# GateLoop and ELU layer on one core: the first unit run straight through, weights converted in single steps, the output layer a round behind, and the rows of w_in permuted

## Chip, cores and metric

The kernel runs on one core of one Trainium2 chip. The metric is the device time of one execution in microseconds (us), the median of several runs. Engine names are those of the profile: PE (TensorE matmul), PEld (its weight load), DVE (VectorE), ACT (ScalarE), POOL (GpSimd), SP (SyncE). The letter q behind a name is the engine's sequencer.

## The reference

A gated linear recurrence with complex gates is followed by a two-layer network with ELU.

```
q, k, v, a_re, a_im : (4, 8, 768, 48) float32;  w_in (384, 2048), w_out (2048, 384) float64
mag = sqrt(a_re^2 + a_im^2);  a = (a_re + i a_im) * min(mag, .999) / (mag + 1e-6)
for t:   S = a_t * S + k_t v_t^T          # S complex, (4, 8, 48, 48)
         y_t = q_t . Re(S)
x   = y as (3072, 384)                    # the 8 heads of 48 side by side
h   = x @ w_in ;  g = where(h > 0, h, exp(min(h, 0)) - 1)
out = g @ w_out                           # (3072, 384) float32
```

## The kernel before

The work is cut into 12 units of 2 x 128 tokens. Per unit the kernel computes log and angle of the gates on ACT and DVE (squares, logarithms, angles), sums them over time with matmuls (turns, decays), takes sines (waves), multiplies q and k (gated), transposes them on PE and forms scores, states and values. The result y is moved by DMA from "two heads of 48 to a block of 64" into the dense layout of x (the seam). Then come 8 pieces of hidden layer and 8 pieces of output layer. A round has 16 slots. In each slot the stages of several units are issued side by side. The account below takes an engine's instructions in their order of issue, as the traces show them at the places that matter: in x_qfirst, the inputs of qg are there by 456.53 us, but qg starts on DVE only at 459.60, behind the g that was issued before it and started at 458.99; in the changed kernel, the squares start on ACT at 503.47, behind the copy of o at 503.09.

The weights are float64 and arrive as pairs of 32-bit words. DVE and POOL make float32 of them:

```python
    def load_weights(dst, src):            # one block of 512 (w_in) or 384 (w_out) columns, 28 blocks
        ...
        nc.sync.dma_start(out=w.rearrange("p n two -> p (n two)"), in_=src)
        lo, hi = w[:, :, 0], w[:, :, 1]
        ...                                                   # four steps on DVE
        nc.gpsimd.tensor_tensor(out=p, in0=p, in1=f, op=ALU.add)
        nc.vector.tensor_scalar(out=hi, in0=hi, scalar1=EXP, ...)
        nc.vector.scalar_tensor_tensor(out=dst, in0=hi, ..., in1=p, ...)

    def gated(u):
        for key, by in (("k", "F"), ("q", "E")):
            g = x[by]
            nc.gpsimd.tensor_tensor(out=g, in0=x[key], in1=g, op=ALU.mult)
            ...
            eng = nc.gpsimd if key == "k" else nc.vector
            eng.tensor_tensor(out=o, in0=g..., in1=x["cs"], op=ALU.mult)      # kg, qg

    def seam(u):                           # ten transfers
        for h in range(H):
            e = 0
            while e < D:
                i, r = divmod(h * D + e, C); n = min(D - e, C - r)
                nc.sync.dma_start(out=x[ds(r, n), i], in_=y[ds(h % 2 * HP + e, n), h // 2])
                e += n
```

The schedule spreads a unit's gate stages over three rounds, and its two layers run in a fourth:

```python
    A = [(1, squares), (4, logarithms), (9, angles), (10, carried)]
    BB = [(2, turns), (4, decays), (9, waves), (10, gated)]
    CC = [...]                             # transposes, scores, states, values; (13, seam)
    M = [hidden(u, f) ... 8 pieces] + [project(u, n, f, f + 4) ... 8 pieces]
    for step in range(NU + 3):
        for s in range(SLOTS):
            for late, stage in ((2, CC), (1, BB), (0, A)):
                u = step - late
                ...                        # the stages of this slot
            if step < 3:
                load_weights(...)          # one block a slot
            if step >= 3:
                M[s](step - 3)
```

## Time and profile before

| | before |
|---|---|
| median of 4 runs | 916.67 us (916.38 to 917.34) |
| span of the profiled run | 918.7 us |
| PE busy / idle | 716.1 / 202.6 us |
| first MLP matmul | 197.4 us |
| a steady round | 62.0 us |

The page, the groups and the chain are read in the prediction below. Two more views of the kernel before will be needed. The first is a table by stretch: length, busy time of each engine with its instructions in brackets, then PE's granted clock (1.00 is full), the DMA share and GB/s.

```profile
0.00:231.39 231.39, 62.43 (x508) 47.83 (x508) 126.16 (x212) 67.50 (x90) 74.38 (x60) 0.69 0.38 88
231.39:880.00 648.61, 621.43 (x4723) 453.82 (x4723) 171.60 (x238) 295.25 (x454) 152.62 (x99) 0.99 0.22 40
```

In the first 231 us PE does 62 us of work. In the next 649, some 10.5 rounds, it is idle for only 27 (2.6 a round) and its mean clock is 0.99.

The second is PE in order of time in a late round: start, length, instruction, and in square brackets the idle time ahead of it with what ended it.

```profile
324.69 0.67 PE L797 MATMUL mlp<-x,w_in 128*128 128x256 f32 x2 [0.69 <-DMA x<-y]
326.67 1.99 PE L797 MATMUL mlp<-x,w_in 128*128 128x256 f32 x8 [1.30 <-DMA x<-y]
```

The idle time of a round lies mostly here, in short pieces: the hidden layer of a unit waits for the transfers of its own seam.

### The profile page before, as it was taken

Reading aid. Unit: us, or ns where it says so; the run is one execution under the profiler, and the core shown is the slowest. Engines: PE = TensorE matmul, PEld = TensorE weight load, DVE = VectorE, ACT = ScalarE, POOL = GpSimd, SP = SyncE. Lnnn points to the kernel's source line nnn. Section 1 sums busy time; section 2 is a strip of 40 time slices with the busy share of each in tenths; the row PEclk is TensorE's granted clock in tenths of the full one; section 3 lists DMA queues with packets and bytes.
Section 4 is the critical chain, followed back from the end, with each engine's and each line's share of the span. In section 5 each row is a group of like instructions: output and inputs, shape, how many; then the busy total and the mean of one; then the engine's idle time right before and its main releaser. Section 6 shows DMA issues by size and latency. Waiting matters only on the chain.

```text
span 918.7 us, 13005 instructions
## 1 busy us (share of the span) xinstructions
PE 716.1 (78%) x5346; PEld 523.7 (57%) x5346; DVE 301.9 (33%) x454; ACT 369.8 (40%) x555; POOL 227.0 (25%) x159
## 2 busy tenths in 40 slices
PE   0100002749999999899999999999999999999997
PEld 0000002538667677576676676776766767778684
DVE  2777875314233232133142331331422312112020
ACT  2310302617437257165273381562733714433040
POOL 1322425222302312313233123132330230110000
PEclk9955556659999999999999999999999999999999
DMA  8243143230142212311411422124113021010100
GB/s 210 60 169 103 20 136 68 37 69 3 34 86 37 48 40 37 76 12 35 87 20 22 83 36 56 33 35 86 25 23 76 3 54 33 2 35 2 35 2 20
DMA packets 177485, 47.04 MB, mean 51 GB/s; under 512 B 165720, under 2 KB 173832, under 8 KB 177416
## 3 DMA queue, kind: packets, MB, share of 16 engines
q1 hardware_dynamic: 177096, 46.09, 24.7%
q8 instruction: 44, 0.72, 0.3%
q14 instruction: 25, 0.20, 0.1%
q0 software_dynamic: 320, 0.03, 0.0%
HBM read 36.55 MB, written 4.79 MB: 45 GB/s over the span
## 4 chain that ended last, share of the span: by engine, by line
PE 48%; POOL 14%; issue 12%; SPq 10%; DVE 10%; DMA 4%; ACT 1%; POOLq 0%; DVEq 0%
PE mlp L797 25%; PE mlp L813 12%; SPq L783 5%; POOL kg L689 4%; SPq L509 3%; POOL wp L553 3%; PE w L704 2%; PE w L712 2%; POOL F L686 2%; POOL E L686 2%; PE w L733 2%; DMA x<-y 2%; DVE wf L543 2%; DVE wp L550 2%; PE y L762 1%
## 5 line engine op out<-in xcount | busy, mean ns | idle before, releaser
L797 PE MATMUL mlp<-x,w_in 128*128 128x256 f32 x1152 | 277.9, 392 | 30.1 <-DMA x<-y 23.6
L797 PEld LDWEIGHTS mlp<-x,w_in 128*128 128x128 f32 x1152 | 218.3, 195 | 73.7 <-issue 18.7
L813 PE MATMUL mlp<-w_out,g 128*128 128x384 f32 x768 | 258.5, 490 | 0.0
L813 PEld LDWEIGHTS mlp<-w_out,g 128*128 128x128 f32 x768 | 143.2, 190 | 92.7
L804 DVE SCALAR_TENSOR_TENSOR g<-ee,mlp 128x512 f32<-128x512 f32 x96 | 64.3, 685 | 271.6 <-ACT ee L803 271.6
L802 ACT ACTIVATE ee<-mlp 128x512 f32<-128x512 f32 x96 | 56.9, 593 | 150.9 <-PE mlp L797 149.1
L704 PE MATMUL w<-ident,qg 128*96 128x128 f32 x192 | 27.2, 288 | 107.6 <-DVE qg L689 107.6
L745 POOL TENSOR_TENSOR S<-S,T 96x384 f32<-96x384 f32 x40 | 33.0, 825 | 273.2 <-DVE S L744 252.4
L819 ACT COPY o<-mlp 128x384 f32<-128x384 f32 x24 | 11.5, 479 | 213.8 <-PE mlp L813 213.8
L704 PEld LDWEIGHTS w<-ident,qg 128*96 128x96 f32 x192 | 21.9, 132 | 112.7 <-DVE qg L689 99.2
L581 POOL TENSOR_TENSOR m<-m,e 128x768 f32<-128x768 f32 x12 | 21.7, 1812 | 175.7 <-ACT e L580 175.7
L803 ACT ACTIVATE ee<-ee 128x512 f32<-128x512 f32 x96 | 60.5, 630 | 2.8
L553 POOL TENSOR_TENSOR wp<-wp,wf 128x384 f32<-128x384 f32 (+1 forms) x28 | 32.1, 1145 | 100.5 <-DVE wp L550 97.6
L628 PE MATMUL w<-th,sum_turns 128*128 128x384 f32 x48 | 19.6, 534 | 43.3 <-ACT th L611 43.3
L689 DVE TENSOR_TENSOR qg<-E,cs 128x1536 f32<-128x1536 f32 x12 | 21.1, 1758 | 93.0 <-POOL E L686 93.0
L733 PEld LDWEIGHTS w<-vn,kg 64*96 64x96 f32 x704 | 37.3, 172 | 17.7 <-issue 9.6
L733 PE MATMUL w<-vn,kg 64*96 64x48 f32 x704 | 40.5, 257 | 7.6 <-DVE z L636 7.6
L597 DVE SCALAR_TENSOR_TENSOR l<-m,e 128x768 f32<-128x768 f32 x12 | 23.6, 1968 | 66.1 <-ACT e L593 66.1
L705 ACT COPY qt<-w 96x512 f32<-96x512 f32 x48 | 25.8, 584 | 40.7 <-PE w L704 40.7
L689 POOL TENSOR_TENSOR kg<-F,cs 128x1536 f32<-128x1536 f32 x12 | 41.6, 3463 | 0.9
L744 DVE TENSOR_TENSOR S<-w,S 96x384 f32<-96x384 f32 x40 | 22.1, 552 | 51.1 <-PE w L733 35.6
L628 PEld LDWEIGHTS w<-th,sum_turns 128*128 128x128 f32 x48 | 9.9, 210 | 47.7 <-ACT th L611 43.3
(65 smaller groups left out, 730.8 us busy)
## 6 DMA issues: line engine op xcount, KB each, us to landing
w<-in_moe_w_in_dram SPq DMA_DIRECT2D x12, 512.0 KB
w<-in_moe_w_out_dram SPq DMA_DIRECT2D x16, 384.0 KB
ar<-in_a_re_dram SPq DMA_DIRECT2D x24, 192.0 KB
ai<-in_a_im_dram SPq DMA_DIRECT2D x24, 192.0 KB
q<-in_q_dram SPq DMA_DIRECT2D x24, 192.0 KB
k<-in_k_dram SPq DMA_DIRECT2D x24, 192.0 KB
vn<-in_v_dram SPq DMA_DIRECT2D x24, 192.0 KB
out_dram<-o SPq DMA_DIRECT2D x24, 192.0 KB
```

The costliest lines, as they stand in the source:

```text
L553: nc.gpsimd.tensor_tensor(out=p, in0=p, in1=f, op=ALU.add)
L686: nc.gpsimd.tensor_tensor(out=g, in0=x[key], in1=g, op=ALU.mult)
L689: eng.tensor_tensor(out=o, in0=g.rearrange("p n h d -> p (n h) d").unsqueeze(2).to_broadcast(shape), in1=x["cs"], op=ALU.mult,)
L704: nc.tensor.transpose(t[:, h], x[key + "g"][:, n, h0 + h], ident)
L733: nc.tensor.matmul(g[:, h], lhsT=x["kg"][ts(c, L), n, h], rhs=vn[u % 2][ts(c, L), n, h, 0:D], start=True, stop=True,)
L745: nc.gpsimd.tensor_tensor(out=new_s, in0=new_s, in1=wide, op=ALU.mult)
L783: nc.sync.dma_start(out=x[ds(r, n), i], in_=y[ds(h % 2 * HP + e, n), h // 2])
L797: nc.tensor.matmul(t[:, e], lhsT=w_in[:, i, ts(f + e, C)], rhs=x["x"][:, i], start=(i == 0), stop=(i == NI - 1),)
L802: nc.scalar.activation(out=e, in_=t, func=AF.Relu, scale=-1.0)
L803: nc.scalar.activation(out=e, in_=e, func=AF.Exp, scale=-1.0)
L804: nc.vector.scalar_tensor_tensor(out=x["g", f // 4][:, f % 4 : f % 4 + 2], in0=e, scalar=-1.0, in1=t, op0=ALU.add, op1=ALU.max)
L813: nc.tensor.matmul(x["o"], lhsT=x["g", f // 4][:, f % 4, ts(n, C)], rhs=w_out[:, f], start=(f == 0), stop=(f == NF - 1),)
```

## The change

The intent is to give PE its first work early and to hide the seam. It has four parts:

1. Unit 0 runs alone and straight through, its POOL products on DVE; weights are converted in its gaps.
2. The conversion is a generator: one DVE instruction at a time, in larger blocks (1024 and 768 columns), with the addition on DVE.
3. A unit goes through all its gate stages in one round, its hidden layer runs in the next, and its output layer half in the one after and half at the start of the one after that. So output pieces of earlier units lie between the seam and the hidden pieces that need it.
4. The rows of w_in are permuted so that 48 of each 64 rows of y are already in place: ACT copies them into x, and six short transfers move the two remaining heads.

```diff
-        nc.gpsimd.tensor_tensor(out=p, in0=p, in1=f, op=ALU.add)
+        yield nc.vector.tensor_tensor(out=p, in0=p, in1=f, op=ALU.add)
 ...
+    def products(u):
+        return nc.vector if u == 0 else nc.gpsimd
 ...
     def seam(u):
-        ...                                            # ten transfers, as above
+        for j in range(2):
+            for i in range(NI):
+                nc.sync.dma_start(
+                    out=x["x"][ds(j * HP + D, G), i], in_=x["y"][ds(j * HP + i * G, G)]
+                )
 ...
-    A = [(1, squares), (4, logarithms), (9, angles), (10, carried)]
-    BB = [(2, turns), (4, decays), (9, waves), (10, gated)]
+    GATE = [
+        (0, squares), (1, logarithms), (3, angles), (3, carried), (4, turns), (5, decays),
+        (6, waves), (7, gated),
+    ]                              # then transposes, scores, states, values in slots 9 to 15
+    GATE.append((SLOTS, seam))
+    MLP = {4 + m: hidden piece m (8 pieces)};  MLP[28 + 4 * n + m] = project piece (8 pieces)
+
+    fetches(1)                     # first block of weights
+    load_qk(0)
+    fetches(1)
+    load_v(0)
+    fetches(1)
+    load_a(1)
+    fetches(1)
+    after = {logarithms: 3, turns: 4, waves: 4, gated: 2}
+    for at, fn in GATE:
+        fn(0)
+        ...
+        converts(after.get(fn, int(9 <= at < SLOTS)))
+    for step in range(NU + 2):
+        for s in range(SLOTS):
+            ...                    # gate stages of unit step + 1
+            if step == 0:
+                fetches(int(s < 8))
+                converts(5 if s < 4 else 3)
+            if step == 1:
+                fetches(s % 2)
+                converts(3)
+            for u, m in ((step - 2, s + 2 * SLOTS), (step - 1, s + SLOTS), (step, s)):
+                if 0 <= u < NU and m in MLP:
+                    MLP[m](u)
```

(Cut: sizes, names and sharing of buffers; two transfers in place of four for the chunk ends; a few short forms in place of loops.) A unit's hidden pieces stand in slots 4 to 11 of its round, its output pieces in slots 12 to 15 of the next round and 0 to 3 of the one after.

## The prediction

Two of its trace readings, in full: at 698.25 us PE's clock went to half for 3.41 us, behind 1.93 us of idle time since 694.84; and 0.42 and 0.69 us (512 columns), 0.35 and 0.56 us (384) are weight steps on DVE in the kernel before, the first of each pair with a constant alone, the second with two tensors.

> **What bounds the kernel now.** I read the page first (busy shares, then the 40 slices), then the chain of waits, then the groups of the first 200 us, then one late round in order of time.
>
> ```profile
> PE 716.1 (78%) x5346; PEld 523.7 (57%) x5346; DVE 301.9 (33%) x454; ACT 369.8 (40%) x555; POOL 227.0 (25%) x159
> ...
> PE   0100002749999999899999999999999999999997
> ...
> DVE  2777875314233232133142331331422312112020
> ...
> PEclk9955556659999999999999999999999999999999
> ```
>
> PE is idle for about nine slices of 23 us, with its clock at half, and is then full to the end. The first 200 us belong to DVE, which makes the float64 weights float32. The groups of these 200 us show the same:
>
> ```profile
> L557 DVE SCALAR_TENSOR_TENSOR w_in<-w,wp 128x512 f32<-128x512 uint32 x12 | 11.5, 956 | 13.8 <-POOL wp L553 13.8
> ...
> L704 PE MATMUL w<-ident,qg 128*96 128x128 f32 x24 | 4.9, 373 | 107.6 <-DVE qg L689 107.6
> ```
>
> Each of the 28 weight blocks hands one addition to POOL and waits for it. In time order, a 512-wide block takes 4.43 us and a 384-wide one 3.58, together 12 x 4.43 + 16 x 3.58 = 110 us. These blocks stand in DVE's order ahead of the gate work of unit 0. PE waits 107.6 us for its first transposes, and the first MLP matmul starts at 197.4.
>
> From there on the chain gives the cost of a round on PE, at full clock:
>
> ```profile
> 607.80 2.58 PE mlp L813 x8
> 610.38 1.08 PE w L712 x32
> ...
> 614.24 1.54 PE w L733 x32
> ...
> 640.16 2.59 PE mlp L797 x12
> 642.75 1.29 PE w L628 x4
> ```
>
> The hidden layer is 8 x 2.59 = 20.7 us, the output layer 8 x 2.58 = 20.6, and the gates 14.9 (transposes 3.8, turns and decays 2.6, scores 2.2, states 3.1, values 3.3): 56.2 us. Successive rounds begin their output layer 62.0 us apart (seven rounds, 297.23 to 731.30). So a round idles 5.8 us, mostly at the seam: "SPq L783" has 5.3% of the chain, ten transfers issued at 0.62 us each.
>
> [...]
> - [...] in the stretches below (PE busy first, granted clock third from the end), some 2 us of idle time in pieces was enough, and the clock came back by 702. After an idle start at 154.0 it fell only at 158.9.
>
> ```profile
> 696.00:698.00 2.00, 0.67 (x2) 0.30 (x2) 0.00 (x0) 0.00 (x0) 0.00 (x0) 1.00 0.26 69
> 698.00:702.00 4.00, 3.85 (x12) 2.99 (x13) 0.00 (x0) 0.16 (x1) 0.00 (x0) 0.57 0.76 148
> 702.00:704.00 2.00, 2.00 (x14) 1.85 (x12) 0.00 (x0) 1.97 (x3) 0.00 (x0) 1.00 0.01 3
> ```
>
> - [...] the 128x1536 product takes 3.46 us on POOL (kg) and 1.76 on DVE (qg).
> - [...] 0.42 us against 0.69 at 512 columns, 0.35 against 0.56 at 384.
> - [...] The trace has the 1283 ns; the next activation begins 1.29 us after the load did[...].
>
> **Part 1: unit 0 straight through.** From the arrival of a_re: ACT starts its squares at 6.2 as now. With the products on DVE (768 columns, 0.82 us each) and no weight block in between, t is ready near 16.5 and the angles at 17.4 (now 43.3). Turns and decays at half clock, the three sines and the four products bring qg to about 35 (now 147). Transposes, scores, states and values at half clock add about 21 us, and the seam (six transfers instead of ten, 3.6 us to issue, 2 to land) puts x at about 61.
>
> **Part 2: the weights.** Scaling the two widths linearly: a constant step costs 0.154 + 0.53 ns a column, the others 0.154 + 1.05. An input part of 1024 is 3 x 0.69 + 4 x 1.23 = 7.0 us, six are 42; an output part of 768 is 3 x 0.56 + 4 x 0.96 = 5.5, eight are 44. That is 86 us against 110, since the addition stays on DVE. Of the 98 steps, 23 lie in unit 0's gaps, 56 in round 0, 19 in round 1. Transfers (12.6 MB at the 233 GB/s of the first 20 us) take 54 us in all and arrive in time.
>
> **Part 3: round 0 and 1.** The order of instructions puts 20 weight steps (20 us) on DVE ahead of the rounding of unit 1's turns, behind a unit 1 that itself waits for ACT and POOL. So hidden's activations start near 84. The other 36 steps (30 us), eight g (5.5) and the gates (7.6) keep DVE to about 127. Round 1 has no output layer ahead of its turns: PE waits some 19 us for the logarithms and the weight steps among them. Work 45.9, two waits of 19 and 5, a cold clock: it ends near 200. By then the new kernel is about 60 us of PE work ahead of the old one, which only begins its first hidden layer.
>
> **Part 4: the steady rounds, where I expect a loss.** The seam now has four output-layer pieces (10.3 us) to hide behind and leaves the path: gain 5.8. But a unit now runs through all its gate stages in one round. Two chains become longer than the PE work beside them.
>
> First: squares stand on ACT behind the copy of o, which waits for the last output-layer piece of slot 15. From there: copy 0.5, squares 1.6, POOL addition 1.8, then the chain that the trace shows from the first logarithm to t:
>
> ```profile
> 656.16 0.84 ACT L589 ACTIVATE m<-m 128x768 f32<-128x768 f32 x1
> ```
>
> ```profile
> 664.32 0.96 DVE L601 SCALAR_TENSOR_TENSOR x<-lr,x 128x768 f32<-128x768 f32 x1 [1.71 <-POOL x L595]
> ```
>
> 9.1 us in all (the two lines are ACT's and DVE's), then arctan 0.85 and the carried row 1.0: 15.1 us. PE has 10.3 us to do before the turns: it waits 4.8.
>
> Second, from the turns: turns 1.3, first hidden piece 2.6, relu, table load and exp 2.6, four E/F 1.6, second piece's relu and exp 1.2, load and three sines 4.0, then kg 3.46 and q*E 1.8 on POOL and qg 1.76 on DVE: 20.5 us. PE has five hidden pieces, turns and decays: 15.6. It waits 5.0. After it, 30.9 us of work runs without a wait that I can find.
>
> A round is then 15.1 + 20.5 + 30.9 = 66.5 us, against 62.0. A wait of 5 us will often halve the clock for one 3.4 us window, sometimes two, losing 2 us: at 0.7 of the waits, 2.8 a round, so 69.3. Six table loads a round instead of four are counted in the chains.
>
> **Sum.** 200 to the end of round 1; 9 x 69.3 = 624; rounds without gates 41.3 + 20.6 + 10.3 = 72; a tail of 6.4 as now (912.3 to 918.7); first and last units' missing states -4: 898. I take 895: the two waits are more likely to overlap with something that I missed than to be longer.
>
> **Rivals.**
> - *PE stays dense.* If ACT, POOL and DVE run ahead so that the two waits shrink to the 5.8 us of now, rounds are 62, and the end is 200 + 558 + 72 + 6 - 4 = 832. For it: all three have much idle time. Against: [...] squares stand behind the o copy.
> - *Everything saved at the start is given back.* If each wait cools the clock for two windows, 3.4 us each, rounds are 73, and the end is about 932. For it: after the gap at 385 the clock stayed low from 387.5 to 394. Against: the three other drops of the steady part lasted about 3.5 us.
> - *DVE bound longer at the start.* If rounds 0 and 1 take 15 us more, from shared waits with POOL (the l step took 1.85 instead of 0.95), the result is about 910.
> - *Transfers late.* Only the fifth and sixth input part are fetched after the first seam; they land near 67 and 71 and are used at 68 and 76. A few us at worst.
>
> **Range and chances.** The start is good to 10 us, the rounds to 2 us each over nine: 868 to 922. The bound for faster by 2% is 898.6, close to my middle: faster 0.53, same 0.43, slower 0.04.
>
> **What would show it.** First MLP matmul near 70 to 77 instead of 197.4; DVE 80% full until about 127; no POOL addition of weights. In a late round two PE waits: before the turns, released by DVE's carried row or ACT's arctan, and before the qg transposes, released by DVE qg, about 5 us each, with half clock after many; none from x. Period 66 to 71. I am wrong if a late round takes under 63 us (the chains overlap in a way that I missed), or if the first output layer is not through by 215 (then DVE or the weights' transfers bound the start).

## The result, and the profile after

The changed kernel takes 941.5 us (median of 4 runs, 940.73 to 941.79) against 916.67 of before. The ratio is 1.0269 (95% interval 1.0251 to 1.0286): slower, and outside the predicted range. Here and below a ratio is the mean time of one kernel's fast runs over that of the other's fast runs in the same rounds, so it is not quite the ratio of the medians. Outputs were right. The profiled run spans 939.7 us at a mean clock of 0.898; before it was 918.7 at 0.912.

The page after, its busy line and its slices of 23.5 us:

```profile
PE 744.2 (79%) x5346; PEld 549.4 (58%) x5346; DVE 311.1 (33%) x390; ACT 400.2 (43%) x600; POOL 186.8 (20%) x125
...
PE   2053772798798798798798799799789789879997
...
PEclk9576795899899899899899989989989989889999
```

PE has exactly as many matmuls as before, 5346, and is busy 28.1 us longer with them (744.2 against 716.1). Its idle time is 195.5 us against 202.6. The span is 21.0 us longer: 28.1 us more for the same matmuls, less 7.1 us of idle time. The slices show where: PE starts early as intended, but then every third slice is a 7, and PEclk dips with it to the end. Before, both were flat. The stretches say the same:

```profile
0.00:231.39 231.39, 126.13 (x1081) 96.42 (x1081) 148.95 (x171) 98.73 (x140) 45.26 (x34) 0.79 0.50 92
231.39:880.00 648.61, 564.68 (x4083) 418.63 (x4084) 157.47 (x209) 293.29 (x446) 141.54 (x91) 0.93 0.19 33
```

At 231 us the new kernel has done 573 matmuls more than the old one. In the next 649 us it does 640 fewer: it is idle for 84 us instead of 27, at a clock of 0.93 instead of 0.99. The head start is gone.

The groups name the waits (busy, mean ns of one, then idle time just before and its main releaser):

```profile
L660 PE MATMUL w<-n,sum_turns 128*128 128x384 f32 x48 | 29.8, 769 | 95.9 <-DVE n L649 63.2
...
L735 PE MATMUL w<-ident,qg 128*96 128x128 f32 x192 | 36.2, 351 | 77.3 <-DVE qg L720 77.3
```

Turns (L660) and qg transposes (L735) hold 173 us of the idle time between them. The hidden layer's matmuls (L827) have 0.0 us of idle time before them, where they had 30.1, of which the transfers of x ended 23.6: the seam is off the path. One late round of PE in order of time:

```profile
518.05 2.25 PE L660 MATMUL w<-n,sum_turns 128*128 128x384 f32 x4 [4.67 <-DVE n L649]
...
540.28 1.94 PE L735 MATMUL w<-ident,qg 128*96 128x128 f32 x8 [4.78 <-DVE qg L720]
...
557.44 0.64 PE L735 MATMUL w<-ident,kg 128*96 128x128 f32 x4 [0.47 <-DVE S L775]
...
589.72 2.25 PE L660 MATMUL w<-n,sum_turns 128*128 128x384 f32 x4 [4.67 <-DVE n L649]
```

The round is 71.67 us long, and holds 9.9 us of idle time in two waits and a small third. The trace records when the clock changes. In stretches cut at these changes, the second wait reads:

```profile
535.79:539.20 3.41, 0.00 (x0) 0.00 (x0) 1.18 (x2) 1.96 (x4) 2.65 (x2) 1.00 0.00 0
539.20:542.61 3.41, 2.33 (x10) 2.17 (x11) 2.22 (x3) 0.93 (x2) 0.00 (x0) 0.50 1.00 180
542.61:546.02 3.41, 3.41 (x10) 2.69 (x9) 0.00 (x0) 0.23 (x1) 0.00 (x0) 0.50 0.35 51
```

The clock is at half for 6.83 us here (539.20 to 546.02), of which 5.74 lie behind the end of the wait at 540.28. Behind the other wait it is at half for 3.41 us (518.72 to 522.13), all of them busy. If work at half clock takes twice as long, the two waits lose 2.87 + 1.71 = 4.58 us a round. This is an estimate from these lengths and the granted 0.50 (the eight qg transposes take 1.94 us here and 1.08 at full clock in x_warm, a factor of 1.8); x_warm below measures the loss.

In the traces of the kernel before and of the changed one, all 15 and 49 changes of the clock lie within 1 ns of a grid of steps of 3.413 us, with its own offset in each trace. In the changed kernel, from 231 us to the last matmuls, 17 full-clock steps held 2.47 us or more of PE idle time, and each was followed by a step at half clock; seven held 1.90 to 1.93 us, and none of these was. In the kernel before, four steps with 1.67 to 2.08 us were followed by one at half clock, and three with 1.52 to 1.57 were not. These are counts of two traces, and no limit is read from them.

Last, the start. The chain of waits of the first stretch, start and length of each link:

```profile
17.66 2.94 PE w L660 x4
...
22.08 7.24 DMA carry<-n
29.40 0.85 ACT n L707
...
36.60 6.35 DMA ends<-n
42.97 0.97 DVE n L717
43.97 1.77 DVE qg L720
```

Turns of unit 0 start at 17.66, near the predicted 17.4. Then two small transfers follow: "carry" (3 KB) takes 7.24 us and "ends" (6 KB) 6.35 us. Both hold the rest up, because the next instruction overwrites what they read (the absolute value in place of the angle, q*E in place of E).

### The profile page after: what moved, and what is told of

Same layout as the page of the kernel before. It is cut to its first block, busy times and chain, and to the rows that moved or that the text cites. A ratio compares the mean times of both kernels' runs of the same rounds, so it can differ in the third digit from the quotient of the medians.

```text
span 939.7 us, 12807 instructions
## 1 busy us (share of the span) xinstructions
PE 744.2 (79%) x5346; PEld 549.4 (58%) x5346; DVE 311.1 (33%) x390; ACT 400.2 (43%) x600; POOL 186.8 (20%) x125
## 4 chain that ended last, share of the span: by engine, by line
PE 51%; issue 12%; DVE 11%; ACT 9%; POOL 6%; DMA 6%; SPq 5%; POOLq 0%; DVEq 0%; ACTq 0%
PE mlp L827 18%; PE mlp L843 16%; PE w L735 6%; SPq L815 3%; PE w L660 3%; PE w L743 2%; POOL n L627 2%; DVE qg L720 2%; DMA vn<-in_v_dram 2%; POOL n L717 2%; PE w L764 2%; PE y L793 2%; ACT ee L832 2%; DMA w<-in_moe_w_in_dram 2%; ACT n L687 2%
## 5 line engine op out<-in xcount | busy, mean ns | idle before, releaser
L827 PE MATMUL mlp<-x,w_in 128*128 128x256 f32 x1152 | 292.8, 415 | 0.0
L827 PEld LDWEIGHTS mlp<-x,w_in 128*128 128x128 f32 x1152 | 244.2, 215 | 47.1 <-issue 5.8
L660 PE MATMUL w<-n,sum_turns 128*128 128x384 f32 x48 | 29.8, 769 | 95.9 <-DVE n L649 63.2
L735 PE MATMUL w<-ident,qg 128*96 128x128 f32 x192 | 36.2, 351 | 77.3 <-DVE qg L720 77.3
L735 PEld LDWEIGHTS w<-ident,qg 128*96 128x96 f32 x192 | 27.4, 161 | 84.3 <-DVE qg L720 75.9
L660 PEld LDWEIGHTS w<-n,sum_turns 128*128 128x128 f32 x48 | 11.3, 258 | 106.5 <-issue 67.4
L801 ACT COPY x<-y 128x384 f32<-128x384 f32 x24 | 11.5, 478 | 137.1 <-PE y L793 137.1
L629 DVE SCALAR_TENSOR_TENSOR n<-n 128x768 f32<-128x768 f32 x12 | 21.1, 1756 | 108.7 <-ACT n L625 108.7
L720 POOL TENSOR_TENSOR kg<-n,cs 128x1536 f32<-128x1536 f32 x11 | 37.9, 3450 | 41.7 <-issue 38.3
L717 POOL TENSOR_TENSOR n<-k,n 128x768 f32<-128x768 f32 x11 | 19.9, 1806 | 72.2 <-ACT n L687 72.2
L736 ACT COPY kt<-w 96x512 f32<-96x512 f32 x48 | 26.4, 577 | 16.0 <-PE w L735 16.0
```

What stands on the lines that cost most here:

```text
L660: nc.tensor.matmul(t, lhsT=sum_turns, rhs=x["th"][:, n].rearrange("p h d -> p (h d)"), start=True, stop=True,)
L717: products(u).tensor_tensor(out=g, in0=x[key], in1=g, op=ALU.mult)
L720: eng.tensor_tensor(out=o, in0=g.rearrange("p n h d -> p (n h) d").unsqueeze(2).to_broadcast(shape), in1=x["cs"], op=ALU.mult,)
L735: nc.tensor.transpose(t[:, h], x[key + "g"][:, n, h0 + h], ident)
L736: nc.scalar.copy(out=o[:, h0 : h0 + 4], in_=t)
L827: nc.tensor.matmul(t[:, e], lhsT=w_in[:, i, ts(f + e, C)], rhs=x["x"][:, i], start=(i == 0), stop=(i == NI - 1),)
```

## The experiments

Two theories were at odds after the result. **The clock**: the waits are as predicted, but each halves the clock for longer than was counted. **Hidden extra work or waits**: something else in the round takes 2.4 us more than 69.3. A third question was the start. The kernels below are the changed kernel with one edit each unless it says otherwise. They ran in three calls on two chips, and the kernel before was run beside them: its medians were 917.48, 917.89 and 918.55 us. The changed kernel itself was not run again; its ratio to before is 1.0269, and comparisons between versions below are of periods in the traces or of these ratios. The outputs of all ten were right.

### x_warm: PE kept busy in the two waits

```diff
+    def warm(u, n):                     # units 2 to 11 only
+        j = ps.tile([C, C // L, 512], FP32, tag="y", bufs=1, name="y")
+        for _ in range(n):
+            nc.tensor.matmul(j[:, 0, 0:256], lhsT=ident, rhs=w_in[:, 0, 0:256], start=True, stop=True)
...
+        if key == "q" and n == 0: warm(u, 9)         # ahead of the qg transposes
...
+        warm(u, 9)                                   # ahead of the turns
```

(Shortened.) The added matmuls compute nothing that is used, and no producer of the real work is touched. They share a PSUM buffer with y, but neither they nor y wait for it in the trace.

> The changed kernel with nine junk matmuls (3.9 us at full clock) put on PE in each of the two waits of a round, before the turns and before the first transposes, for units 2 to 11; they read finished weights and write an unused part of PSUM. My account of a round of 71.67 us: 56.2 work, waits of 4.67, 4.78 and 0.47, and about 5.2 lost because PE's clock is halved for 3.4 to 6.8 us after each of the two waits (I had put 2.8 for this). If so, the waits' lengths on the chain stay, the low clock goes, a round takes 66 to 67 us and the kernel about 890 us. Rival: the slow stretch after a wait is not the idle time's doing[...]: then the round stays at 71 or more and the time at 940 or more.

Measured: 896.61 us (896.18 to 897.9), ratio 0.9768 [0.973, 0.9807]. One late wait on PE in order of time, and, one round earlier, the stretch behind the same wait:

```profile
516.21 1.08 PE L749 MATMUL w<-ident,qg 128*96 128x128 f32 x8 [0.92 <-DVE qg L722]
```

```profile
448.00:452.00 4.00, 3.08 (x19) 2.73 (x19) 2.18 (x3) 1.07 (x2) 0.00 (x0) 1.00 0.98 183
```

The round is 67.17 us. Nine added matmuls take 4.05 us and 0.92 is left of the wait: together 4.97, so the chain that ends at qg is as long as before (4.78). Only the clock has changed. It is 1.00, and the same eight transposes take 1.08 us instead of 1.94. More work made the kernel about 45 us faster, some 4.5 us in each of ten rounds, close to the estimate of 4.58. The clock theory is shown. The other falls: what is left, 67.17, is within a microsecond of the 66.5 of the prediction's sum without a clock penalty, and 0.47 of the difference is the small third wait.

### x_warm5: fewer added matmuls

```diff
-WARM_T, WARM_Q = 9, 9
+WARM_T, WARM_Q = 5, 5
```

> As the run with junk matmuls in both waits of a round, but five instead of nine (2.2 us at full clock), so that some 2.5 us of each wait stay idle. The full junk gave 896.6 us and a round of 67.17 without low clock, none gave 941.5 and 71.67. [...] If an idle stretch of some 2.5 us is enough often (in the kernel before, about 2 us in pieces was enough four times in nine), part of the loss stays: 905 to 930 us.

Measured: 908.57 us (906.49 to 909.99), ratio 0.9877 [0.9832, 0.9921]. The five matmuls take 2.32 us and leave 2.44 us idle before the turns and 2.64 before the transposes. Two stretches that each begin about when the turns do, in two successive rounds:

```profile
504.00:508.00 4.00, 3.56 (x15) 2.77 (x16) 2.62 (x5) 0.00 (x0) 0.00 (x0) 1.00 0.83 174
...
572.00:576.00 4.00, 4.00 (x11) 2.71 (x10) 2.23 (x4) 0.00 (x0) 0.41 (x1) 0.57 0.98 202
```

The idle time ahead of both is 2.44 us. Behind the first the clock stays full, behind the second it is near half. So with these shorter waits the penalty comes in some rounds and not in others, and not behind the three longer waits of 2.64 us from 435 to 600 us (before 457.88, 525.03 and 593.88; the eight transposes behind each take 1.08 us). The clock changes at 572.07 and 575.48. In steps of 3.413 us counted from there, the wait before 571.60 lies whole in one step (568.66 to 572.07), the one before 504.44 has 1.80 us in one step and 0.64 in the next, and the one before 525.03 has 1.89 and 0.75. The result lies between x_warm and the changed kernel.

### x_early: squares and logarithms in the round before

```diff
-        (0, squares), (1, logarithms), (3, angles), ...
+        (-3, squares), (-2, logarithms), (3, angles), ...
-            for late, shift in ((0, SLOTS), (1, 0)):
+            for late, shift in ((0, SLOTS), (1, 0), (2, -SLOTS)):
```

Squares stand in slot 13 of the round before, no longer behind the copy of the finished output. In the changed kernel ACT shows that order:

```profile
503.09 0.48 ACT L849 COPY o<-mlp 128x384 f32<-128x384 f32 x1 [2.12 <-PE mlp L843]
503.47 0.85 ACT L611 ACTIVATE n<-ar 128x768 f32<-128x768 f32 x1
```

> The changed kernel with squares and logarithms of a unit moved three slots back into the round before (slots 13 and 14 instead of 0 and 1), nothing else. My account: the wait before the turns (4.67 us, and some 1.8 us of half clock) exists because the chain from squares to the carried row takes 15 us and starts behind the o copy with 10.3 us of PE work left. Started three slots earlier it has over 20 us: the first wait goes, a round takes about 65 us, the kernel about 865 us. Rival: ACT, POOL and DVE are so full in slots 13 to 15 (values, scores, states) that the chain delays these instead: a round stays above 69 and the time above 920.

Measured: 881.31 us (879.3 to 882.49), ratio 0.9602 [0.9564, 0.964].

```profile
485.19 1.45 PE L660 MATMUL w<-n,sum_turns 128*128 128x384 f32 x4
505.67 1.94 PE L735 MATMUL w<-ident,qg 128*96 128x128 f32 x8 [4.79 <-DVE qg L720]
```

The turns no longer wait and run at full clock (1.45 us instead of 2.25). The second wait is as it was. The round is 64.86 us, 6.8 shorter than 71.67: the wait of 4.67 plus 2.1 us of clock. The first wait's cause, that the logarithm chain begins only behind the copy of o, is shown.

### x_qfirst: the products of q ahead of those of k

```diff
-        for key, by in (("k", "F"), ("q", "E")):
+        for key, by in (("q", "E"), ("k", "F")):
```

POOL then makes q*E before it makes kg, which takes 3.46 us.

> The changed kernel with the order of the gated products swapped: q*E and qg before k*F and kg, nothing else. My account: the wait before the first transposes (4.78 us, and some 2.9 us of half clock after it) exists because qg stands behind kg's 3.45 us and k*F's 1.8 us on POOL. With q first, qg is ready before PE gets to it, kg still in time for its own transposes: the second wait goes, a round takes about 64 us, the kernel about 860 us. Rival: the wait only moves to kg's transposes 3.6 us of PE work later, or to the store of the chunk ends that reads E before it is overwritten: then a round loses less than 3 us and the time stays above 910.

Measured: 916.72 us, ratio 0.998 [0.9939, 1.002]; round 68.26 us. The wait shrank from 4.78 to 2.84 us and did not vanish. The round lost 3.4 us where 7.7 were expected, and the time is the rival's (above 910), though the cause is neither of the two that the rival named. All engines in order of time tell why:

```profile
458.33 0.63 ACT L833 ACTIVATE ee<-ee 128x512 f32<-128x512 f32 x1
...
458.99 0.69 DVE L834 SCALAR_TENSOR_TENSOR g<-ee,mlp 128x512 f32<-128x512 f32 x1 [5.74 <-ACT ee L833]
...
459.60 2.13 DVE L720 TENSOR_TENSOR qg<-n,cs 128x1536 f32<-128x1536 f32 x1
...
461.78 1.94 PE L735 MATMUL w<-ident,qg 128*96 128x128 f32 x8 [2.84 <-DVE qg L720]
```

The product qg stands in DVE's order behind the g of a hidden piece. That g waits 5.74 us for an exp, and the exp stands on ACT behind two sines, the absolute value between them and a table load of 1.28 us (the recorded texts count three sines). With POOL out of the way, a second chain of nearly the same length ends the wait.

### x_both: the two edits together

The diff is the sum of the last two.

> The changed kernel with both repairs: squares and logarithms three slots earlier and q's products before k's. The two alone gave 881 and 917 against 941.5 us; the round was 71.67 us as changed, 68.26 with q first and 64.86 with the early squares, which are 21, 20 and 19 times 3.413 us. With q first a wait of 2.84 us is left (qg stands on DVE behind the g of hidden piece 2, whose exp stands on ACT behind the sines). So together: work 56.2, that wait of about 2.8, the 0.47 before kT, and a cold clock after some of the waits only: a round of 60 to 61.4 us (18 windows of 3.413 would be 61.4), and 881 - 10 x 4 = about 840 us. Rival (the two waits are not separate: removing one lengthens the other): a round of 64 and 870 us or more.

Measured: 858.48 us (856.18 to 862.45), ratio 0.9352 [0.931, 0.9393]. The round is 62.0 us with one wait of 2.84 us (3.19 in the first round shown). Behind it the eight transposes take 1.26 to 1.94 us in all seven rounds from 246 to 626 us, against 1.08 at full clock. Three of these were cut finer: the clock is at half for 3.41 us from 374.85 and from 436.29, and for 6.83 from 497.73. The expected 840 us had it fall after some of the waits only. Two small edits, neither of which removes any work, turn the change from 2.7% slower to 6.5% faster. The gains of the two single edits (6.7 and 2.9 points of the ratio) nearly add up to the 9.2 found together.

### x_start: weights fetched behind the small transfers of unit 0

```diff
-    load_v(0)
-    fetches(1)
-    load_a(1)
-    fetches(1)
 ...
     for at, fn in GATE:
         fn(0)
+        if fn is decays:
+            load_v(0)
+            fetches(1)
+            load_a(1)
+            fetches(1)
```

> The changed kernel with v of unit 0, weight part 2, a of unit 1 and weight part 3 issued after unit 0's decays instead of before its squares. My account of the 16 us by which the start came later than I predicted: qg of unit 0 (45.7 instead of 35) waits until the 6 KB store of the chunk ends, issued at 36.6 and landed at 42.97, has read E, because 3 MB of weights and inputs stand ahead of it on the sync queue. Moved behind it, qg is ready near 36 and everything after it 8 to 9 us earlier: about 932 us. Rival: DVE's weight steps set the start anyway (PE waited 8.7 us for the rounding of unit 1 behind them), so that the time moves by under 3 us.

Measured: 931.64 us (931.04 to 933.23), ratio 1.0152 [1.0111, 1.0192].

```profile
35.27 1.94 PE L735 MATMUL w<-ident,qg 128*96 128x128 f32 x8 [12.18 <-DVE qg L720]
```

The first transposes start at 35.27 instead of 45.78; "ends" now takes 1.73 us from issue to landing instead of 6.35. The gain of about 10 us stays to the end: turns of the third and fourth unit start at 149.09 and 220.82, in the changed kernel at 159.21 and 231.39. So 10 of the 16 us that the start missed were these two transfers behind the bulk of the weights. Most of it is not the transfer itself: SP issues "ends" at 24.47 us, in the changed kernel only at 36.60, after the loads that stand before it. The other 6 were not taken apart. A candidate, not shown, is DVE: the 98 weight steps took 95.5 us in the changed kernel instead of the predicted 86, and the nine longest (1.5 to 2.6 us) all ran while a POOL instruction did (the longest of the 67 that did not took 1.23).

### y_seam: the kernel before with part 4 alone

```diff
-        x["y"] = new("y", 1, [C, NP, GT])
+        x["x"], x["y"] = new("x", 2, [C, NI, GT]), new("y", 1, [C, GT])
 ...                                        # two copies and six transfers, as in the change
-            (w_in[:, i, f : f + WC], moe_w_in[ts(i, C), ...])
+            (w_in[:, i, f : f + WC], (i, words * f, words * (f + WC)))    # permuted rows
```

> The kernel before with one part of the change: w_in's rows permuted so that three of four head pairs are copied straight into x and only six transfers of 16 rows remain, in place of ten transfers; schedule, weights' steps and all else as before. My account: in the kernel before a round of 62.0 us has 56.2 of work, and most of its idle 5.8 us is the wait of hidden for x (23.6 us in the table over the rounds, plus the half clock after some of them). With four transfers less (2.5 us of issue) most of it goes: a round of 58 to 59.5 us and 875 to 895 us. Rival: the wait moves to qg or to g, as these were nearly as late: 905 us or more.

Measured: 890.63 us (889.2 to 891.52), ratio 0.9703 [0.9675, 0.973]. Rounds take 58.43 us instead of 62.0. From 231 to 850 us PE is idle for 7.6 us and its clock is 1.00. Of the waits only two short ones are left:

```profile
451.97 0.91 PE L656 MATMUL w<-l,sum_logs 128*128 128x384 f32 x2 [0.20 <-DVE S L750]
...
464.87 2.86 PE L802 MATMUL mlp<-x,w_in 128*128 128x256 f32 x12 [0.67 <-DVE g L809]
```

Part 4 is sound by itself: it is worth 27 us, 3%. What the whole change lost must come from the other three parts, or from how the parts act together.

### x_near: the output layer in its own round

```diff
-                if 0 <= u < NU and m in MLP:
+                if 0 <= u < 2 and m in MLP:
                     MLP[m](u)
+            for u, m in ((step - 1, s + SLOTS), (step, s)):
+                if 2 <= u < NU:
+                    m += SLOTS * (m >= 12)     # pieces after slot 11 come a round later, as a whole
+                    if m in MLP:
+                        MLP[m](u)
```

> The changed kernel with the output layer of units 2 to 11 in the unit's own round (slots 12 to 15 and 0 to 3 of the next), so that one part of the change, the output layer a round behind, is undone where the weights allow it. My account: the same number of output-layer pieces stands in the same slots, so both waits (4.67 and 4.78 us) and the round of 71.67 us stay: 941 us, within 5. Rival: g of the last hidden piece is not ready when the output layer starts, and PE waits 2 us or more in every round, or the other way round the later layer costs something: the time moves by more than 10 us.

Measured: 934.88 us (933.9 to 935.04), ratio 1.0186 [1.016, 1.0211]. Both waits (4.67 and 4.78) and the round (71.6) are as in the changed kernel. The 6.6 us are fewer than the changed kernel's time but more than was expected of this edit; the round in which the two orders meet holds extra output pieces. Where the output layer's pieces come from, this unit or the one before, is not what makes the steady rounds long.

### z_front and z_front2: all gate stages moved forward

```diff
-        (0, squares), (1, logarithms), (3, angles), (3, carried), (4, turns), (5, decays), (6, waves), (7, gated),
+        (-5, squares), (-3, logarithms), (-1, angles), (-1, carried), (0, turns), (1, decays), (3, waves), (4, gated),   # z_front
+        (-4, squares), (-2, logarithms), (-1, angles), (-1, carried), (2, turns), (3, decays), (4, waves), (5, gated),   # z_front2
```

Both include the edits of x_qfirst and x_start. The second also has three weight steps in each slot of round 0 instead of five in the first four slots.

> A version meant to be better than both: the changed kernel with the front of the gate chain taken apart again, squares at slot -5, logarithms -3, angles -1, turns 0, decays 1, waves 3, products 4 (q first), transposes still at 9; and the small transfers of unit 0 ahead of the weights as in the run that gave 931.6. Between squares and turns lie about 17 us of PE work and 10 us more of other work, between turns and the transposes 23 us against chains of 15.1 and 20.5: both waits go, with the clock losses after them, and so do the waits for unit 1's and unit 2's turns at the start (8.7, 15 and 21 us in the changed kernel). A round of 57 us, the end of round 1 near 176 instead of 216, in sum 176 + 9 x 57 + 72 + 6 = about 767 us. Rival: with PE full, ACT or DVE in-order waits take the place, a round of 60 or more: over 800 us.

Measured: 862.42 us (857.46 to 864.83), ratio 0.9378 [0.9335, 0.9421], far from what was hoped. Two new waits took the place of the old ones. In each round PE waits for POOL:

```profile
523.54 1.81 POOL L626 TENSOR_TENSOR n<-ar,n 128x768 f32<-128x768 f32 x1 [8.35 <-ACT n L624]
525.43 2.39 POOL L627 TENSOR_TENSOR n<-ai,n 128x768 f32<-128x768 f32 x1
...
530.23 1.74 PE L793 MATMUL y<-qt,S 96*48 96x64 f32 x28 [3.66 <-POOL S L776]
```

The two products of the logarithms, moved into slot 13, now stand on POOL just ahead of the products of the states, and the carried chain of states reaches PE 3.66 us late. And in round 0, with the gates early, the hidden layer stood behind 20 weight steps on DVE: one wait of 22.40 us, and another of 13.19 in the next round.

> The better version again, with the two new waits of the last one mended. There the logarithms' two POOL products stood ahead of the state products of the same round, so that values waited 3.66 us for S (round 63 to 64 us), and unit 1's first g stood behind 20 weight steps (22.4 us). Now squares at slot -4, logarithms at -2 (behind the states of slot 14), angles -1, turns 2, decays 3, waves 4, products 5, and three weight steps a slot in round 0 instead of five in its first four. Waits left in a round: 0.47 before kT and perhaps 1 us: 57 to 58.5 us without low clock; end of round 1 near 180: 180 + 9 x 58 + 78 = about 780 us. Rival: an in-order wait that I haven't seen takes the place again: a round of 61 or more and over 820 us.

Measured: 797.68 us (797.5 to 799.07), ratio 0.8677 [0.864, 0.8715]. This is the fastest version, 13% faster than the kernel before. Its slices:

```profile
PE   1456682789999999999999999999999999999996
...
PEclk9676895889999999999999999999999999999999
```

From about 180 us on PE is full. The clock is 1.00 from 200 to 700 us, and 0.9 or more in every slice of the page from 179 us on. A round takes 57.9 us, of which only 0.47 is a wait. PE is busy 708.6 us with its 5346 matmuls, 36 less than in the changed kernel.

No run has the changed kernel with the old seam. What parts 1 to 3 would cost alone stays open.

## Why the prediction was wrong

It said 895 (868 to 922) and gave "slower" a chance of 0.04; 941.5 came, slower. Point by point:

- **What bounds the kernel** was right: PE at full clock has 56.2 us of work a round. With the clock kept up, x_warm's round less its waits and added matmuls is 67.17 - 10.2 = 57.0.
- **The seam** leaves the path: right (0.0 us of idle time on L827). Its size was not: "a round idles 5.8 us" was got by subtracting modelled work from the period. The trace has 2.6 us of idle time a round before, and y_seam gains 3.6 a round.
- **The weights**: right in kind. Steps at 1024 columns take 0.69 and 1.22 to 1.31 us, none are on POOL, and there is no wait on a weight transfer in the steady part. In all they took 95.5 us, not 86, and DVE was 72% full to 127 us, not 80%.
- **The two waits**: right in place, releaser and size. Before the turns 4.67 us against 4.8, before the qg transposes 4.78 against 5.0. A third, 0.47, was not seen. x_early and x_qfirst confirm both chains, the second only in part: the sum was computed through POOL, and a second chain through ACT and DVE, only 1.9 us shorter, was not looked for. The sizes are in part luck: the listed terms add up to 14.9 and 20.3 us, not 15.1 and 20.5, and the work left over is 56.2 - 10.3 - 15.6 = 30.3, not 30.9. So 66.5 is 1.0 too high for its own terms, and the real work, 71.67 - 9.92 - 4.58 = 57.2, was 1.0 above the listed 56.2.
- **The step that failed first** is "A wait of 5 us will often halve the clock for one 3.4 us window, sometimes two, losing 2 us: at 0.7 of the waits, 2.8 a round". Both waits halved it in every steady round, the first for 3.41 us (eight times from 232.00 to 733.76) and the second for 6.83 (eight times from 252.48 to 754.24). The clock cost 4.5 us a round by the difference to x_warm (4.58 by the estimate from the trace), not 2.8. The period is 71.67, not 69.3: of the 2.4 us, 1.8 are the clock, 0.5 the work and 0.1 the waits. On nine rounds the period's error is 9 x 2.4 = 21 us. The prediction's own rival, "each wait cools the clock for two windows", with rounds of 73 and 932 us, came nearest in number. Half of its mechanism is right (the second wait), and its total is near partly by luck, since it leaves out the late start. It was set aside because three drops in the kernel before lasted only 3.4 us. But these came behind 1.7 to 2.0 us of idle time each, in pieces. The fourth came behind 2.08 us, had another 1.13 us of idle time inside it (387.71 to 388.84), and lasted 6.83. So this one, a gap that reached into the low stretch, was the better guide to the wait of 4.78 us, which reached 1.08 us into its own.
- **The step that failed second** is the start: "brings qg to about 35" and "it ends near 200". The transposes started at 45.78, and round 1 ended at 216.4. The chain of instructions was right: with the two small transfers free, x_start has 35.27. What was missing is that "ends" and "carry" must have been read before their source is overwritten, while the queue in front of them holds v, the next gates and two blocks of weights. The rival "Transfers late" looked only at the weights themselves. This is 10 of the 16 us; the other 6 stay open.
- **The sum** with the two terms as measured: 216.4 + 9 x 71.67 + 72 + 6.4 - 4 = 936, against a span of 939.7. Either error alone (21 or 16 us) would have left the result inside the range. The rest, 4 us, and the 3 us that were rounded down from 898 to 895, are not worth a cause. (Its bound for faster by 2%, 898.6, should be 0.98 x 916.67 = 898.3.)
- **What would show it wrong** was named as rounds under 63 us or a first output layer later than 215. The second came true: the first output layer (unit 0's, 199.58 to 226.71) was not through by 215, and the weights' transfers were a part of the reason, though through the small transfers behind them. The other error was not on the list: rounds longer than the stated 66 to 71.

Why the change is slower on balance: it wins a head start of 573 matmuls, about 60 us as predicted. It also takes the seam off the path, which is worth 27 us on the old schedule (y_seam). Then it puts a unit's whole gate chain into one round, and makes two chains longer than the PE work that covers them. That makes a round 9.7 us longer (71.67 - 62.0, the gain of the seam already taken off), and over nine or ten rounds this is more than the head start. Of the 9.7 us, 7.3 are idle time (9.9 against 2.6 before) and 2.4 are longer matmuls, as a net figure: the low clock costs 4.6 a round now (4.58 by the estimate above) and some 0.8 before (the same estimate: 17.1 us at half clock in 10.5 rounds), and what shortened the matmuls by the rest was not looked into. Idle time and clock are not independent: x_warm, which gives PE something to do in the waits, takes off 4.5.

## What to carry to other kernels

Put every wait of the busiest engine into the sum twice: once as idle time and once for the clock that the trace shows lowered behind it (here 9.9 us of idle time and about 4.5 us of clock a round), and measure the second by filling the wait with matmuls that do nothing, checking that the waits keep their length. Before a stage is moved, write down what stands ahead of it on every engine, and look for the second-longest chain as well, since removing one releaser can uncover the next (x_qfirst: 4.78 us of wait became 2.84, not 0). Small transfers whose source is about to be overwritten belong ahead of bulk loads in the order of issue (x_start: "ends" took 1.73 us instead of 6.35).

## More that the traces show

- The rounds of three versions whose clock falls in each round of the trace are near whole multiples of 3.413 us: the changed kernel's 71.67 is 21.0 of them, x_qfirst's 68.26 is 20.0, x_early's 64.86 is 19.0. That of x_both, 62.0, is 18.2. No run tests whether the one has to do with the other.
- "Carry" was issued from POOL and took 7.24 us for 3 KB, while SP's queue was loading weights; "ends", 6 KB on the sync queue, took 6.35 us behind bulk loads, and 1.73 us in x_start without them.
- A table load on ACT takes 1.28 us. In the kernel before, the load at 168.76 us began 0.02 us after the activation before it ended, and the next activation began 1.30 us after the load did; behind the load at 171.65 it was 1.29.
